# Expert weights loaded in other places, the first transposes copied amid the bias rows, one exponential for the last keys' bias, and more bias rows on ScalarE

## The chip, the cores and the metric

The kernel runs on one core of one Trainium2 chip. The metric is the time of one execution in device microseconds (us). TensorE is called PE here, its weight loads PEld, VectorE DVE, ScalarE ACT, GpSimd POOL; SP is the engine whose queue issues plain and transposing DMAs.

## The reference, cut to what matters

Attention over 8 sequences with 8 heads, 576 positions and 64 values a head, with a bias made of the distance of two positions; each row of the result (4,608 rows of 512 values) then goes through one of 8 experts, chosen by its domain.

```python
rel = pos[:, None] - pos[None, :]
x = (log1p(abs(rel)) / log1p(max(pos[:, None], 1)))[..., None]
bias = relu(x @ w1 + b1) @ w2                     # 576 x 576 x 8 heads
scores = q @ k.T / 8 + bias                       # for each sequence and head
rows = softmax(scores) @ v                        # 4608 x 512 after a transposition
for e in range(8):
    out[domain == e] = relu(rows[domain == e] @ moe_w1[e]) @ moe_w2[e]
```

## The kernel before, in words

**The bias.** It is the same for all sequences and made once, as its exponential. There are nine blocks: `hidden(ib)` makes 16 rows `hr` (each a 128x576 relu) on DVE (L202) or ACT (L199), and `outputs(ib)` multiplies them on PE with `W2BIG` into three PSUM tiles: query groups (0, 1) and (2, 3), 32 matmuls each (L221), and the last 64 keys, 16 matmuls (L225). ACT then takes exponentials into `biasM` (L237) and, for the last keys, into `biasR` (L234, two of them, one for each parity of the heads). `hidden(ib + 1)` is written ahead of `outputs(ib)`, so the rows of a block are made while PE works on the block before it. The ninth block is taken in pieces between score units of the first sequence (`LAST_ROWS`). Some fifty small routing operations of DVE (`next(route)`) also lie in this stretch and in the first sequence.

**The attention.** One round of `ROUND` for each sequence sets the order on PE, ACT and DVE by hand. A score unit (`m01`: head pair 0, key group 1) is two to eight matmuls into a ring of three PSUM tiles and one exponential on ACT (L560); `W..` multiplies by the bias on DVE (L571), `A..` multiplies with v on PE (L584, L588), `N.` divides by the sums on DVE (L614, L615). `T01`, `T23` transpose q and k of the next sequence on PE (L476), and `D..`, that is `take`, copies them out of PSUM (L506, on DVE). Those of the first sequence are made within the bias: (4,) after block 5, (0, 1) after block 6, (2, 3) after block 7, all through the one accumulator tile `pu`.

**The rows.** Rows of the result are scattered to a buffer in HBM, `fire_x`, sorted by expert (L645, on POOL: four DMAs of 128 rows, `xt`, and one of 64, `xl`, for each sequence). The scatters of a sequence are issued in the round after it.

**The experts.** An expert's weights are four quarters `w`, each 512 KB in SBUF after a cast in the DMA (L737, on POOL). There are 32; they go to a pool of 12 (`w_first`), to five of six tiles that held q, k and v (`n4`), and to a pool of 14 (`w_late`), whose first tile is used twice. `xA` is the first 512 rows of expert 0, fetched by a transposing DMA on SP before the last sequence is through (L952); `xT` are the other rows, expert by expert (L788, three buffers), and `ids` their destinations (L790). For each expert PE makes eight pairs of matmul groups (L799; expert 0: L809 with `xA`, L817 with the rest), ACT takes the relu (L839), PE multiplies with the second weights in five `second`s (L775, 40 matmuls), DVE copies each to a `res` tile (L778, eight buffers), and POOL scatters it to the output (L779).

**What sets the order.** POOL issues its DMAs strictly in the order in which they are written (`_Issue`), and a DMA of POOL waits for the one eight before it to have landed, since eight semaphores are used in turn. SP's queue is in order too. The calls `G.w.load(n, ...)` in `late` (by sequence `b` and unit number `ui`), at the head of `_phase_moe` and after each `second` say where the quarters stand in POOL's order.

Of the kernel before, what the change touches and what calls it, by code (L numbers as in the profile page):

```python
# [10 lines left out]
F16 = mybir.dt.float16  # L11
# [19 lines left out]
NSLOT = E * CAP + 128 * NOVF  # L31
PAD = 1 << 20
LN_EXP = 6
XW = DM + 2


# [25 lines left out]
""".split()  # L62


LAST_ROWS = {"m01": 1, "m03": 1, "m11": 2}


def rap(t, off, dims, nparts=None):
# [115 lines left out]
def _phase_bias(tc, G, route, at, x_dram):  # L184
# [4 lines left out]
    def hidden(ib, between=None):  # L189
        hrl = []  # L190
        for k16 in range(16):
            if ib < 8:
                r, a = ib // 2, 16 * (ib % 2) + k16
                m, c0 = 32 * r + a, C4 - (16 * a + r)
            else:
                m, c0 = 128 + k16, W4 + C1 - 4 * k16
            hr = fsb.tile([P, S], F16, tag="hr", name="hr", bufs=34)
            if k16 in ((2, 5, 8, 11, 14) if ib < 2 else (3, 8, 13) if ib % 2 == 0 else (5, 11)):
                nc.scalar.activation(out=hr, in_=G.L4[:, c0: c0 + S], func=AF.Relu,  # L199
                                     bias=G.pb1[:], scale=G.slope[:, m: m + 1])  # L200
            else:
                nc.vector.tensor_scalar(out=hr, in0=G.L4[:, c0: c0 + S],  # L202
                                        scalar1=G.slope[:, m: m + 1], scalar2=G.nb1[:],
                                        op0=AO.mult, op1=AO.max)
            hrl.append(hr)
            if (ib, k16) == (0, 7):
                G.slopes(16, NGR)
            if (ib, k16) in ((1, 1), (1, 5), (1, 9), (2, 1), (2, 5)):
                next(route)
            if between is not None and k16 == between[0]:  # L210
                at.take(0, between[1])
        return hrl

    def outputs(ib, hrl):
        for jcs in ((0, 1), (2, 3), (4,)):
            eb = G.ring()
            for k16 in range(16):
                for lj, jc in enumerate(jcs):
                    hr = hrl[k16]
                    if jc < 4:  # L220
                        nc.tensor.matmul(out=eb[:, lj, 32 * k16: 32 * k16 + 32],  # L221
                                         lhsT=rap(hr, jc, [[4, 128]]),
                                         rhs=G.W2BIG[:, 0:32], start=True, stop=True)
                    else:
                        nc.tensor.matmul(out=eb[0:64, lj, 32 * k16: 32 * k16 + 32],  # L225
                                         lhsT=hr[:, 512:576],
                                         rhs=G.W2BIG[:, 0:32], start=True, stop=True)
            ebv = eb.rearrange("p l (i h) -> p l h i", h=8)
            i0 = 64 * ib
            if jcs[0] == 4:  # L230
                for h2 in range(2):
                    o = G.biasR[64 * h2: 64 * h2 + 64, :, i0: i0 + 64] if ib < 8 else \
                        G.biasRL[64 * h2: 64 * h2 + 64]
                    nc.scalar.activation(out=o, in_=ebv[0:64, 0, h2::2, :],  # L234
                                         func=AF.Exp, bias=0.0, scale=0.125)
            elif ib < 8:
                nc.scalar.activation(out=G.biasM[:, jcs[0]: jcs[0] + 2, :, i0: i0 + 64], in_=ebv,  # L237
                                     func=AF.Exp, bias=0.0, scale=0.125)
# [10 lines left out]

    hrl = hidden(0)  # L250
    for ib in range(9):
        after = hidden(ib + 1, {6: (3, (4,)), 7: (9, (0, 1))}.get(ib)) if ib < 8 else None
        if ib == 1:
            nc.vector.memset(G.zero.rearrange("p o (r d) -> p (o r) d", r=4)[:, :, DM:].bitcast(I32), PAD)
            nc.sync.dma_start(out=x_dram.rearrange("(p c r) d -> p c (r d)", p=P, r=4),
# [3 lines left out]
                yield  # L259
        if ib == 0:  # L260
            next(route)
        if ib in (5, 6, 7):
            ps = {5: (4,), 6: (0, 1), 7: (2, 3)}[ib]
            at.transposes(0, ps, G.acc())
        if ib == 7:
            yield
        hrl = after
# [143 lines left out]
class _Attention:  # L411
# [85 lines left out]
    def take(self, b, ps):  # L497
        asb = self.G.asb
        if ps == (4,):
            t = self.qkTl[b] = asb.tile([P, 4, 2, 128], F16, tag="qkTl", name="qkTl", bufs=2)  # L500
            self.nc.vector.tensor_copy(out=t, in_=self.pt.pop((b, 4)))
        else:
            t = asb.tile([P, 2, 2, 512], F16, tag="qkT", name="qkT", bufs=4)
            for i, p in enumerate(ps):
                self.qkT[b, p] = t[:, i]
            self.nc.vector.tensor_copy(out=t.rearrange("p i x f -> p i (x f)"),  # L506
                                       in_=self.pt.pop((b, ps)).bitcast(F16))

    def scores(self, b, u):
        nc, G = self.nc, self.G  # L510
# [146 lines left out]
            self.load_vrag(b)  # L657

    def run(self, bias, route, late):
        units = [("r", 0)] + [("m", p, c) for p in (0, 1) for c in range(4)] + [("r", 1)] + \  # L660
                [("m", 2, c) for c in range(4)] + [("l", 0), ("l", 1), ("x",)] + \
                [("m", 3, c) for c in range(4)]
# [7 lines left out]
        def unit(b, name):  # L670
# [4 lines left out]
            if b == 0 and name in LAST_ROWS:  # L675
                for _ in range(LAST_ROWS[name]):
                    next(bias, None)
            if (b, name) == (0, "m00"):
                self.take(0, (2, 3))
            if b == 0 and ui > 2:  # L680
                for _ in range(2):
# [85 lines left out]
def _phase_moe(tc, G, moe_w1, moe_w2, x_dram, out):  # L767
# [50 lines left out]
                                 rhs=xT[:, dc, EARLY:], start=(dc == 0), stop=(dc == 3))  # L818
        nc.scalar.activation(out=hT[:, :, EARLY:], in_=hps, func=AF.Relu, bias=0.0, scale=1.0)

    G.w.load(2, G.n4)
    G.w.load(2, G.w_late)
    xTs = {e: fetch(e) for e in range(2)}
    novf = None
    for e in range(E):
# [62 lines left out]
def kernel(  # L888
# [24 lines left out]
    with tc.manual_schedule(engines={ET.PE, ET.DVE, ET.Activation}):  # L913
        with ExitStack() as att:
# [23 lines left out]
            def late(b, ui):  # L938
                if (b, ui) == (0, 7):
# [1 line left out]
                    G.bias_pools.close()  # L941
                    wsb = ctx.enter_context(tc.tile_pool(name="wsb", bufs=1, side="right", reuse_waits="tile"))
                    G.w_first = lambda name: wsb.tile([P, 2048], F16, tag="w", name=name, bufs=12)
                if b < 6 and ui == 10:
                    G.w.load(1, G.w_first)
                if (b, ui) in ((6, 1), (7, 5)):
                    G.w.load(3, G.w_first)
                if (b, ui) == (6, 3):
                    G.w.load(3, G.n4)
                if (b, ui) == (B - 1, 9):  # L950
                    G.early = G.n4("xA").rearrange("p (c t) -> p c t", c=4)
                    nc.sync.dma_start_transpose(out=G.early, in_=x_dram[0: EARLY, 0:DM])  # L952
# [36 lines left out]
```

## Time and profile before

| | |
|---|---|
| median of 3 runs | 398.47 us (397.8 to 398.48) |
| the profiled execution | 398.14 us, of which 396.6 us are the span from the first to the last instruction |
| busy in the span | PE 324.9 us (82%), ACT 246.9 (62%), DVE 236.6 (60%), PEld 214.2 (54%), POOL 182.5 (46%) |
| mean granted clock of TensorE | 0.956 of full speed |

The profiled execution is 1.54 us longer than its span and 0.33 us under the median. A share of busy time is a mean over three stages that have little in common: the bias to about 54 us, the attention to about 222 us, the experts to the end.

### The profile page before, as it was taken

To read this page: it belongs to the slowest core of one execution; us is meant where nothing else is said; L and a number is where in the kernel's file an instruction comes from. 1 tells how busy PE (TensorE), PEld (TensorE's weight loads), DVE (VectorE), ACT (ScalarE), POOL (GpSimd) and SP (SyncE) were. 2 spreads that over 40 slices of the span, in tenths; PEclk is the share of its full clock that TensorE was granted. 3 is DMA by queue.
4 is the path that set the end of the run, shared out by engine and by line. 5 is a ranking of instruction groups with operands and counts; after the bars stand their busy time and mean duration, and the time that the engine had idled before them with its cause. 6 is when DMAs were issued, how large, how long until landed. Compare 5 with 4: busy or idle time off the path is not lost.

```text
span 396.6 us, 9316 instructions
## 1 busy us (share of the span) xinstructions
PE 324.9 (82%) x3938; PEld 214.2 (54%) x3938; DVE 236.6 (60%) x440; ACT 246.9 (62%) x302; POOL 182.5 (46%) x220
## 2 busy tenths in 40 slices
PE   1599968789898989898787493999969985999893
PEld 1477846656566666565555243555536542656551
DVE  7999986999999999999889400212211202031211
ACT  8999968699999999999899040333214220514230
POOL 9250033049696969696445070836410046040312
PEclk9999988899999999999999697999989998999997
DMA  5999999039999999999966959999999259130302
GB/s 90 176 189 367 373 263 182 4 38 170 133 165 135 163 140 164 132 167 135 199 139 123 132 108 186 192 201 228 227 216 222 56 83 276 40 116 5 126 26 96
DMA packets 90996, 61.30 MB, mean 155 GB/s; under 512 B 43462, under 2 KB 85190, under 8 KB 90953
## 3 DMA queue, kind: packets, MB, share of 16 engines
q0 software_dynamic: 59904, 45.12, 69.2%
q1 hardware_dynamic: 31048, 15.57, 17.5%
q8 instruction: 31, 0.51, 0.5%
q14 instruction: 13, 0.10, 0.1%
HBM read 61.93 MB, written 24.70 MB: 218 GB/s over the span
## 4 chain that ended last, share of the span: by engine, by line
issue 24%; DVE 21%; DMA 19%; ACT 15%; PE 12%; POOL 6%; SPq 1%; POOLq 1%; DVEq 0%
ACT e L560 14%; DVE hr L202 7%; DMA out_dram<-res,ids 7%; DVE e L571 6%; POOL out_dram L779 5%; PE pu L588 4%; DMA w<-in_moe_w_dram 4%; DMA xA<-fire_x 3%; DMA ids<-fire_x 3%; DVE xt L615 2%; PE sc L532 2%; DVE qkT L506 2%; PE sc L476 2%; PE sc L538 1%; PE pu L584 1%
## 5 line engine op out<-in xcount | busy, mean ns | idle before, releaser
L560 ACT ACTIVATE e<-sc 128x1024 f16<-128x1024 f32 x168 | 152.2, 1019 | 13.1 <-PE sc L532 5.6
L778 DVE COPY res<-ops 128x512 f32<-128x512 f32 x40 | 27.6, 691 | 137.9 <-PE ops L775 126.8
L839 ACT ACTIVATE hT<-hps 128x640 f16<-128x640 f32 x56 | 39.4, 703 | 93.2 <-PE hps L799 76.1
L775 PE MATMUL ops<-w,hT 128*128 128x512 f16 x320 | 72.9, 387 | 5.3 <-DVE res L778 5.3
L571 DVE TENSOR_TENSOR e<-e,biasM 128x2048 f16<-128x2048 f16 x64 | 72.9, 1150 | 0.6 <-ACT e L560 0.4
L779 POOL DMA_INDIRECT out_dram<-res,ids x40 | 40.5, 1012 | 68.5 <-DVE res L778 48.7
L799 PE MATMUL hps<-xT,w 128*128 128x320 f16 x448 | 63.7, 304 | 5.3 <-DMA xT<-fire_x 4.3
L799 PEld LDWEIGHTS <-w 128*128 128x128 f16 x448 | 44.2, 99 | 25.2 <-issue 5.7
L532 PE MATMUL sc<-qkT 64*128 64x512 f16 x256 | 45.1, 385 | 15.0 <-ACT e L560 13.8
L775 PEld LDWEIGHTS <-hT 128*128 128x128 f16 x320 | 31.8, 100 | 43.6 <-issue 8.5
L645 POOL DMA_INDIRECT fire_x<-xt,posi x32 | 46.6, 1457 | 12.0 <-issue 8.2
L588 PE MATMUL pu<-vext,e 128*128 128x65 f16 x1024 | 48.1, 196 | 4.0 <-DVE e L571 4.0
L588 PEld LDWEIGHTS <-e 128*128 128x128 f16 x1024 | 43.4, 99 | 6.9 <-DVE e L571 5.0
L737 POOL DMA_DIRECT2D w<-in_moe_w_dram x32 | 27.7, 943 | 37.6 <-PE hps L799 32.2
L202 DVE TENSOR_SCALAR hr<-L,slope,nb 128x576 f16<-128x576 f16 x116 | 41.5, 427 | 0.0
L221 PE MATMUL sc<-W2BIG,hr 128*128 128x32 f16 x576 | 27.7, 193 | 13.1 <-DVE hr L202 9.6
L645 POOL DMA_INDIRECT fire_x<-xl,posi x8 | 10.4, 1296 | 52.8 <-DVE e L571 40.3
L221 PEld LDWEIGHTS <-hr 128*128 128x128 f16 x576 | 23.2, 116 | 17.8 <-DVE hr L202 14.1
L532 PEld LDWEIGHTS <-qkT 64*128 64x128 f16 x256 | 12.2, 93 | 35.5 <-issue 29.2
L584 PE MATMUL pu<-vrag,e 128*128 128x130 f16 x128 | 28.6, 223 | 2.2 <-DVE xl L631 1.4
L615 DVE TENSOR_TENSOR xt<-pu,rz 128x512 f16<-128x512 f32 (+1 forms) x33 | 22.3, 675 | 1.5
L199 ACT ACTIVATE hr<-L,pb,slope 128x576 f16<-128x576 f16 x28 | 22.2, 858 | 1.0 <-DVE slope L165 0.8
(128 smaller groups left out, 365.9 us busy)
## 6 DMA issues: line engine op xcount, KB each, us to landing
w<-in_moe_w_dram POOLq DMA_DIRECT2D x32, 512.0 KB
fire_x<-zero SPq DMA_DIRECT2D x1, 9252.0 KB
qn<-in_q_dram POOLq DMA_DIRECT2D x8, 512.0 KB
kn<-in_k_dram POOLq DMA_DIRECT2D x8, 512.0 KB
vst<-in_v_dram POOLq DMA_DIRECT2D x8, 512.0 KB
out_dram<-res,ids POOLq DMA_INDIRECT x40
last<-zero SPq DMA_DIRECT2D x2, 256.0 KB
last<-in_q_dram POOLq DMA_DIRECT2D x16, 32.0 KB
```

The source lines that it names most:

```text
L202: nc.vector.tensor_scalar(out=hr, in0=G.L4[:, c0: c0 + S], scalar1=G.slope[:, m: m + 1], scalar2=G.nb1[:], op0=AO.mult, op1=AO.max)
L221: nc.tensor.matmul(out=eb[:, lj, 32 * k16: 32 * k16 + 32], lhsT=rap(hr, jc, [[4, 128]]), rhs=G.W2BIG[:, 0:32], start=True, stop=True)
L532: mm(out=sc[:, h2, :], lhsT=self.qkT[b, p][hs[h2], 1, 128 * c: 128 * c + 128], rhs=self.qkT[b, p][hs[h2], 0, :], start=not raw, stop=True)
L560: nc.scalar.activation(out=ef[:, 0:n], in_=sf[:, 0:n], func=AF.Exp, bias=0.0, scale=0.125)
L571: self.nc.vector.tensor_tensor(out=job[0], in0=job[0], in1=job[1], op=AO.mult)
L584: mm(out=self.pu[:, c // 2, o: o + 130], lhsT=er[:, p % 2, 128 * c: 128 * c + 128], rhs=vr[:, p, :], start=True, stop=False, skip_group_ch ...
L588: mm(out=self.pu[:, c // 2, o + 65 * h2: o + 65 * h2 + 65], lhsT=self.e[b, ("m", p, j)][:, h2, 128 * c: 128 * c + 128], rhs=vx[:, 2 * p + ...
L645: inst = self.nc.gpsimd.indirect_dma_start(out=self.x_dram[:, :], out_offset=bass.IndirectOffsetOnAxis(ap=self.G.posi[0:n, c:c + 1], axis= ...
L775: nc.tensor.matmul(out=ops_, lhsT=hT[:, fc, t0: t0 + 128], rhs=G.w.w2(e, fc), start=(fc == 0), stop=(fc == 7))
L779: inst = nc.gpsimd.indirect_dma_start(out=out[:], out_offset=bass.IndirectOffsetOnAxis(ap=idx.bitcast(I32), axis=0), in_=res[:], in_offset ...
L799: nc.tensor.matmul(out=hps[:, i, 0:HC], lhsT=G.w.w1(e, dc, fc), rhs=xT[:, dc, HC * hf: HC * hf + HC], start=(dc == 0), stop=(dc == 3))
L839: nc.scalar.activation(out=hT[:, fc, :].rearrange("p (a b) -> p a b", a=2), in_=first(e, xT, ((fc, 0), (fc, 1))), func=AF.Relu, bias=0.0, ...
```

## The change

It has five parts. (1) The quarters of the weights stand elsewhere in POOL's order. Unit 10 of sequences 0 to 6 loads 4, 2, 1, 2, 1, 1 and 1 (it was one in each of sequences 0 to 5); three still go to `n4` at unit 3 of sequence 6, two more now at its unit 13. The three at unit 1 of sequence 6, the three at unit 5 of sequence 7 and the four at the head of `_phase_moe` are gone. So 17 quarters stand ahead of the experts where 15 and then four stood, and 15 behind `second`s where 13 did. (2) The first sequence's copy of (0, 1) stands after 2 rows of the ninth block, not 10; its transposes (2, 3) and their copy stand behind the score unit m01, not after block 7; the ninth block's pieces follow m03, m10 and m11, not m01, m03 and m11. (3) The last keys' matmuls are 32 of 16 columns, even heads to partitions 0 to 63 and odd heads to 64 to 127, and one exponential takes both. (4) Blocks 3, 5 and 7 give ACT three rows each instead of two. (5) The second transposes of sequence 1 are copied on ACT.

```diff
+W_FIRST = {0: 4, 1: 2, 2: 1, 3: 2, 4: 1, 5: 1, 6: 1}
-LAST_ROWS = {"m01": 1, "m03": 1, "m11": 2}
+LAST_ROWS = {"m03": 1, "m10": 1, "m11": 2}
...
-            if k16 in ((2, 5, 8, 11, 14) if ib < 2 else (3, 8, 13) if ib % 2 == 0 else (5, 11)):
+            if k16 in ((2, 5, 8, 11, 14) if ib < 2 else (3, 8, 13)):
...
-                        nc.tensor.matmul(out=eb[0:64, lj, 32 * k16: 32 * k16 + 32],
-                                         lhsT=hr[:, 512:576],
-                                         rhs=G.W2BIG[:, 0:32], start=True, stop=True)
+                        for h2 in range(2):
+                            nc.tensor.matmul(out=eb[64 * h2: 64 * h2 + 64, 0, 16 * k16: 16 * k16 + 16],
+                                             lhsT=hr[:, 512:576],
+                                             rhs=rap(G.W2BIG, h2, [[2, 16]]), start=True, stop=True)
...
-                for h2 in range(2):
-                    o = G.biasR[64 * h2: 64 * h2 + 64, :, i0: i0 + 64] if ib < 8 else \
-                        G.biasRL[64 * h2: 64 * h2 + 64]
-                    nc.scalar.activation(out=o, in_=ebv[0:64, 0, h2::2, :],
-                                         func=AF.Exp, bias=0.0, scale=0.125)
+                nc.scalar.activation(out=G.biasR[:, :, i0: i0 + 64] if ib < 8 else G.biasRL,
+                                     in_=eb[:, 0, 0:256].rearrange("p (i q) -> p q i", q=4),
+                                     func=AF.Exp, bias=0.0, scale=0.125)
...
-        after = hidden(ib + 1, {6: (3, (4,)), 7: (9, (0, 1))}.get(ib)) if ib < 8 else None
+        after = hidden(ib + 1, {6: (3, (4,)), 7: (1, (0, 1))}.get(ib)) if ib < 8 else None
...
-        if ib in (5, 6, 7):
-            ps = {5: (4,), 6: (0, 1), 7: (2, 3)}[ib]
-            at.transposes(0, ps, G.acc())
+        if ib in (5, 6):
+            at.transposes(0, (4,) if ib == 5 else (0, 1), G.acc())
...
+            if (b, ps) == (1, (2, 3)):
+                self.nc.scalar.copy(out=o, in_=i)
+            else:
+                self.nc.vector.tensor_copy(out=o, in_=i)
...
-            if (b, name) == (0, "m00"):
+            if (b, name) == (0, "m01"):
+                self.transposes(0, (2, 3), G.acc())
                 self.take(0, (2, 3))
...
-    G.w.load(2, G.n4)
-    G.w.load(2, G.w_late)
     xTs = {e: fetch(e) for e in range(2)}
...
-                if b < 6 and ui == 10:
-                    G.w.load(1, G.w_first)
-                if (b, ui) in ((6, 1), (7, 5)):
-                    G.w.load(3, G.w_first)
-                if (b, ui) == (6, 3):
-                    G.w.load(3, G.n4)
+                if ui == 10 and b in W_FIRST:
+                    G.w.load(W_FIRST[b], G.w_first)
+                if (b, ui) in ((6, 3), (6, 13)):
+                    G.w.load(3 if ui == 3 else 2, G.n4)
```

On POOL, from the scatters of sequence 6 to the first outputs, this stood before (`fire_x` is the row buffer, `out_dram` the output):

```order
L645 DMA fire_x<-xt,posi 9216x514 x4
L737 DMA w_4362<-in_moe_w_dram 128x4x512
L737 DMA w_4364<-in_moe_w_dram 128x4x512
L737 DMA w_4366<-in_moe_w_dram 128x4x512
L639 IOTA xt 128x4
L639 IOTA xl 64x1
L645 DMA fire_x<-xl,posi 9216x514
L645 DMA fire_x<-xt,posi 9216x514 x4
L737 DMA w_4677<-in_moe_w_dram 128x4x512
L737 DMA w_4679<-in_moe_w_dram 128x4x512
L737 DMA w_4681<-in_moe_w_dram 128x4x512
L737 DMA w_4683<-in_moe_w_dram 128x4x512
```

At the same place of the changed kernel stands:

```order
L647 DMA fire_x<-xt,posi 9216x514 x4
L641 IOTA xt 128x4
L641 IOTA xl 64x1
L647 DMA fire_x<-xl,posi 9216x514
L647 DMA fire_x<-xt,posi 9216x514 x4
L783 DMA out_dram<-res,ids 4608x512
L741 DMA w_4893<-in_moe_w_dram 128x4x512
L783 DMA out_dram<-res,ids 4608x512
```

The three loads behind sequence 6's scatters and the four behind sequence 7's are gone from there; the first load among the experts now stands behind the first output.

On POOL, at unit 10 of sequence 0, one load stood between the counters of the rows (IOTA) and the first scatter; in the changed kernel there are four:

```order
L641 IOTA xt 128x4
L641 IOTA xl 64x1
L741 DMA w_1683<-in_moe_w_dram 128x4x512
L741 DMA w_1685<-in_moe_w_dram 128x4x512
L741 DMA w_1687<-in_moe_w_dram 128x4x512
L741 DMA w_1689<-in_moe_w_dram 128x4x512
L647 DMA fire_x<-xl,posi 9216x514
```

The first scatter of sequence 0 and the loads of q and k of sequence 3 behind it now follow four loads.

On ACT, from the last full block of the bias into the first sequence, this stood before (`e` are the exponentials of scores, a number marks the tile that two units share):

```order
L199 ACTIVATE hr<-L_110,pb_89,slope 128x576 x3
L237 ACTIVATE biasM<-sc 128x16x64 x2
L234 ACTIVATE biasR<-sc 64x4x64 x2
L560 ACTIVATE e<-sc 128x1024
L560 ACTIVATE e_1288<-sc 128x1024 x2
L244 ACTIVATE biasL<-sc 128x4x2x64 x2
L560 ACTIVATE e_1336<-sc 128x1024 x2
L244 ACTIVATE biasL<-sc 128x4x2x64 x2
L560 ACTIVATE e_1391<-sc 128x1024 x2
L234 ACTIVATE biasRL<-sc 64x256 x2
```

Now stands there, down to the copy of part (5):

```order
L233 ACTIVATE biasR<-sc 128x4x64
L562 ACTIVATE e<-sc 128x1024
L562 ACTIVATE e_1375<-sc 128x1024 x2
L562 ACTIVATE e_1421<-sc 128x1024 x2
L244 ACTIVATE biasL<-sc 128x4x2x64 x2
L562 ACTIVATE e_1476<-sc 128x1024
L244 ACTIVATE biasL<-sc 128x4x2x64 x2
L562 ACTIVATE e_1476<-sc 128x1024
L233 ACTIVATE biasRL<-sc 128x256
L562 ACTIVATE e_1604<-sc 128x1024 x2
L562 ACTIVATE e<-sc 128x1024
L562 ACTIVATE e_1677<-sc 128x1024 x2
L507 COPY qkT<-sc 128x2048
```

Five exponentials of scores now come before the first piece of the ninth block, and a copy of 2,048 elements stands among those of the third head pair.

## Rows read from the trace of the kernel before

**Rows 1.** Busy time by stage: attention, first expert, experts 1 to 4.

```profile
core 0: us, PE busy (x) PEld busy (x) DVE busy (x) ACT busy (x) POOL busy (x), PEclk, DMA share, GB/s
82.00:222.50 140.50, 118.85 (x2048) 83.25 (x2044) 132.07 (x191) 131.85 (x147) 98.02 (x108) 1.00 1.00 146
222.50:253.80 31.30, 21.06 (x105) 10.79 (x105) 4.89 (x12) 5.12 (x5) 12.91 (x14) 0.79 0.94 147
253.80:336.40 82.60, 73.05 (x418) 41.55 (x417) 13.82 (x20) 22.50 (x32) 30.51 (x33) 0.96 1.02 190
```

**Rows 2.** Timeline of PE among the experts: start, length, instructions, [idle before, releaser].

```profile
221.89 0.60 PE L588 MATMUL pu<-vext,e 128*128 128x65 f16 x8
226.10 8.36 PE L809 MATMUL hps<-xA,w 128*128 128x512 f16 x32 [3.61 <-DMA xA<-fire_x]
234.30 3.62 PE L775 MATMUL ops<-w,hT 128*128 128x512 f16 x16
244.55 3.60 PE L817 MATMUL hps<-xT,w 128*128 128x128 f16 x32 [6.63 <-DMA xT<-fire_x]
253.76 8.86 PE L799 MATMUL hps<-xT,w 128*128 128x320 f16 x64
271.81 8.85 PE L799 MATMUL hps<-xT,w 128*128 128x320 f16 x64 [0.56 <-DMA xT<-fire_x]
293.01 10.53 PE L799 MATMUL hps<-xT,w 128*128 128x320 f16 x64 [3.71 <-DMA xT<-fire_x]
312.01 8.86 PE L799 MATMUL hps<-xT,w 128*128 128x320 f16 x64
331.32 5.20 PE L775 MATMUL ops<-w,hT 128*128 128x512 f16 x16 [5.28 <-DVE res L778]
336.36 8.86 PE L799 MATMUL hps<-xT,w 128*128 128x320 f16 x64
353.69 8.86 PE L799 MATMUL hps<-xT,w 128*128 128x320 f16 x64
```

**Rows 3.** Timeline of POOL, around the last scatters and the last load.

```profile
211.44 2.69 POOL L737 DMA_DIRECT2D w<-in_moe_w_dram  x3
...
226.88 0.95 POOL L645 DMA_INDIRECT fire_x<-xl,posi  x1 [12.49 <-DMA xA<-fire_x]
...
232.99 3.44 POOL L737 DMA_DIRECT2D w<-in_moe_w_dram  x4
...
321.17 0.76 POOL L737 DMA_DIRECT2D w<-in_moe_w_dram  x1 [32.19 <-PE hps L799]
```

**Rows 4.** DMA issues: queue, count, us from issue to landing.

```profile
xA<-fire_x SPq DMA_TRANSPOSE x1, 12.8
```

**Rows 5.** Timeline of DVE, the last division of the attention.

```profile
222.75 0.42 DVE L615 TENSOR_TENSOR xt<-pu,rz 128x256 f16<-128x256 f32 x1
```

**Rows 6.** DMA queues, 280 to 284 us: packets, MB, share of 16 engines.

```profile
q0 software_dynamic: 601, 0.78, 92.1%
q1 hardware_dynamic: 599, 0.15, 27.1%
```

**Rows 7.** DMA queues, 304 to 308 us.

```profile
q1 hardware_dynamic: 3750, 0.91, 115.3%
```

**Rows 8.** Busy time, clock and DMA from 70 to 82 us.

```profile
70.00:82.00 12.00, 9.81 (x142) 7.51 (x141) 11.86 (x19) 8.43 (x10) 0.00 (x0) 0.86 0.00 1
```

**Rows 9.** Timeline of DVE in the bias and the first sequence.

```profile
28.16 4.51 DVE L202 TENSOR_SCALAR hr<-L,slope,nb 128x576 f16<-128x576 f16 x13
...
64.42 1.22 DVE L506 COPY qkT<-sc 128x2048 f16<-128x2048 f16 x1 [2.64 <-PE sc L476]
...
72.23 1.22 DVE L506 COPY qkT<-sc 128x2048 f16<-128x2048 f16 x1
```

**Rows 10.** Timeline of ACT there.

```profile
50.20 0.75 ACT L234 ACTIVATE biasR<-sc 64x256 f16<-64x256 f32 x2
54.84 2.85 ACT L560 ACTIVATE e<-sc 128x1024 f16<-128x1024 f32 x3 [3.89 <-PE sc L538]
...
74.33 1.02 ACT L560 ACTIVATE e<-sc 128x1024 f16<-128x1024 f32 x1 [2.85 <-PE sc L545]
```

**Rows 11.** Timeline of PE, the last keys' matmuls of one block.

```profile
29.40 1.04 PE L225 MATMUL sc<-W2BIG,hr 128*64 128x32 f16 x16
```

More of the change, by code (lines that the diff above doesn't have):

```diff
@@ L505, in take @@
                 self.qkT[b, p] = t[:, i]
-            self.nc.vector.tensor_copy(out=t.rearrange("p i x f -> p i (x f)"),
-                                       in_=self.pt.pop((b, ps)).bitcast(F16))
+            o, i = t.rearrange("p i x f -> p i (x f)"), self.pt.pop((b, ps)).bitcast(F16)
+            if (b, ps) == (1, (2, 3)):
+                self.nc.scalar.copy(out=o, in_=i)
+            else:
+                self.nc.vector.tensor_copy(out=o, in_=i)
     def scores(self, b, u):
@@ L659, in run @@
     def run(self, bias, route, late):
+        G = self.G
         units = [("r", 0)] + [("m", p, c) for p in (0, 1) for c in range(4)] + [("r", 1)] + \
```

## The prediction

> **What bounds the kernel now.** I read the busy time by stage first. In the attention, 82 to 222.5 us, ACT is busy for 131.85 of 140.5 us, DVE for 132.07 [rows 1]. That stage is bound by its engines, and the change leaves its instructions as they are. Among the experts only PE could bind, and there it loses time twice: it is busy for 21.06 of 31.30 us with expert 0 and for 73.05 of 82.60 us with experts 1 to 4, and the granted clock falls to 0.79 and 0.96 of full speed, so part of that is PE at the lower of its two levels [rows 1]. The timeline of PE says what it waits for [rows 2]: 3.61 us for `xA`, 6.63 us for expert 0's other rows, 0.56 and 3.71 us for the rows of experts 2 and 3, 5.28 us for a result tile. An undisturbed expert takes 353.69 - 336.36 = 17.33 us; the steps before it take 18.05, 21.20, 19.00 and 24.35 us.
>
> What is late behind these waits stands on POOL and in the queues. Three quarters of weights are issued at 211.44 us, just ahead of `xA`, which then takes 12.8 us to land [rows 3, 4]. The last sequence's scatters wait 12.49 us for `xA` to have been read, since they write the same buffer. Behind them come four more quarters at 232.99 us, and the fetch of expert 0's other rows starts amid these. The last quarter waits 32.19 us for a tile, and every output behind it waits too [rows 3].
>
> **The change part by part.** A quarter is 0.524 MB. With both queues full, POOL's queue q0 moved 0.78 MB in 4 us, so a quarter costs 2.7 us of it [rows 6].
>
> (1) `xA`, -3.6 us. Without the three quarters it has the queues almost to itself. Its 0.52 MB would take 2.3 us at the 0.91 MB in 4 us that q1 moved alone [rows 7]. With a start and an end of 1 to 2 us I estimate 5 us, where it took 12.8. PE has it at 226.10, so it is issued near 213.3 us, 9 us before PE ends the attention at 222.49 [rows 2]; the whole 3.61 us go; the other bound is nothing, if the 12.8 us have another cause.
>
> (2) Expert 0's other rows, -7.9 us. The five scatters take 232.99 - 226.88 = 6.1 us of POOL. They can begin when `xA` has been read, at about 220 us; the last two wait for the division that ends at 223.17 us [rows 5]. I put their end at 226.5 us, 6.5 us earlier, and the fetch with it at about 228. No load is in flight then, so 128 rows land in 3 us or so, by 231. PE comes there at 222.49 + 8.36 + 3.62 = 234.5 us, so 6.63 us of wait go, with 3 us to spare. The stretch from 244.55 to 253.76 us is 9.21 us, begun at the lower clock after that idle time. At full clock its 24 second matmuls are 24 of the 40 that take 17.33 - 8.86 = 8.47 us, so 5.1; the 32 short ones I put between 1.8 (half of 3.60) and 3.6, near 2.9. That gives 8.0 and -1.2. Bounds 0 and -8.6. Expert 1 begins near 242.2.
>
> (3) Experts 1 to 3, -6.3 us: three steps at 17.33 are 52.0 where 58.25 stand (253.76 to 312.01). This holds if each `xT` lands in time. From 228 us q1 runs alone until POOL has issued the first output and the first load behind it. That is when PE's first `second` is through and copied, near 233.5, so the load's data come near 236. In 8 us q1 alone moves 1.8 MB; expert 0's rest, expert 1 and half of expert 2 are 1.1. The remaining half then goes at 0.15 MB in 4 us [rows 6], 9 us, to 245, and is wanted at 259.5. Expert 3's rows, 17.5 us each at that pace, come near 263, wanted at 276.9; expert 4's near 281, wanted at 294.2. Bounds 0 and -6.3.
>
> (4) Expert 4, -7.0 us. Before, the last quarter stands behind expert 2's third `second`; seven results are queued behind it, of eight tiles. Now it stands behind the fifth, and five are queued, so three tiles are free when expert 4's `second`s start. The first tile came back at most 331.32 - 321.17 = 10.15 us after POOL went on [rows 2, 3]; the fourth result of expert 4 would then be copied some 3 us late, on DVE. PE has two PSUM tiles for results and then 8.86 us of expert 5's first matmuls, so it doesn't wait. 24.35 becomes 17.33. Bounds 0 and -7.0.
>
> (5) The bias and the first sequence, -3.5 us. DVE gives up three rows of 4.51 / 13 = 0.35 us, 1.0 us together, and a copy of 1.2 us at 72.23; a wait of 2.64 us at 64.42, for transposes that stand behind pieces of the ninth block, should shrink as ACT starts earlier [rows 9]. From 70 to 82 us DVE is busy for 11.86 of 12 us [rows 8], so what DVE gains here carries to the first full round. ACT's first score exponential waits 3.89 us, idle, for matmuls behind the copy that moves [rows 10]. ACT takes on three rows, the copy (two exponentials of 1,024 would be 1.9 us) and loses nine of 0.38 us; it has 3.89 and 2.85 us of idle time to hold that. DVE's certain part is 2.2, with all of the wait 4.8; I take half of the wait. Low end: +1.0, if the copy of 1.9 us on ACT delays scores and the wait stays.
>
> The last keys' matmuls are part of that bound. 16 took 1.04 us [rows 11]; 32 of half the width take between 1.04 and 2.08. PE waits for rows of DVE in every block, so only those of the last full block stand ahead of the first score unit: 0 to +1.0 us. The Trainium skill (TensorEngine Tiling (Array Packing), Instruction Overhead) says that a matmul of one column lasts as long as one of 60; by it the 32 take 2.08 us, and the sum is 1.0 us longer. The same page (Key Properties) lets different column tiles work in parallel, which would give 1.04 and change nothing; no row of this trace shows halves of 16 columns.
>
> The moved loads I cost at nothing. In sequence 0 three more are 8 us of q0; the DMA engines do nothing from 72 to 82 us, and POOL has nothing to issue [rows 8]. In sequences 1 and 3 one more is 2.7 us in a round of 20 (140.5 us hold seven); the DMA share is 1.00 there and 1.19 with both queues full [rows 1, 6], some 3 us free in a round. What these loads could delay, q, k and v, is wanted a round later. Without that cover each costs 2.7 us.
>
> Sum: -3.6 - 7.9 - 6.3 - 7.0 - 3.5 = -28.3; 398.14 - 28.3 = 369.8, and against the median, 0.3 above the profiled execution, 370.1 us.
>
> **The rivals.**
> *The transposes stay starved.* Packets of q0 and q1 go one for one, 601 to 599, and q1's are a fifth as large [rows 6]; experts 2 and 3 were 21.2 us apart, near the 17.5 us of one fetch. If loads fill q0 before expert 1's rows are in, that pace holds for two steps: 2 x (21.2 - 17.33) = +7.7, 377.8 us. Against it: q1 has 8 us to itself. The Trainium skill (DMA: Bandwidth & Descriptors, Queues, rings and completion order) says that each engine takes queues in turn, packet by packet; the trace agrees, 601 to 599. By that rule alone any step with loads in flight goes at 21 us.
> *The last quarter still stops the outputs.* If its tile or the results come back later than I think, (4) gives nothing: 377.1 us.
> *Only expert 0 gains.* If (3), (4) and half of (5) fail together, because 15 loads behind `second`s are two more than before and keep q0 full: 398.5 - 11.5 - 1.7 = 385.3 us.
> *Slower.* Loads beside q, k and v make the attention wait for DMA. To cost more than the 28 us, each of seven rounds would have to be 4.1 us longer, more than a load's 2.7. The DMA share of 1.00 leaves too little backlog for that, unless POOL, in order and eight DMAs deep, falls a whole round behind.
>
> **How the numbers follow.** Forecast 0.58, range 365 to 374 from the ends of (5) and a miss of 3 us among the experts. Transposes 0.17, last quarter 0.08, only expert 0 0.10, no change 0.02, slower 0.05. A measurement of this kernel tells 0.2%, 0.8 us, from no change. So faster 0.93, within 0.2% 0.02, slower 0.05. 365 to 380 us holds the first three, 0.83.
>
> **What would show it.** `xA` landing in about 5 us and no idle time of PE before L813's group of `xA` (L809 before); the other rows' matmuls without a wait; experts 17.3 us apart throughout; no idle PE in expert 4; the first score exponential near 51 us; an attention of 140 us from its second sequence on, as before. The prediction is wrong if a round grows by 2 us or more, if expert 1's rows land after 243 us, or if PE waits for a result tile.

## The result and the profile after

The changed kernel took 372.98 us as a median of four executions (367.99 to 390.59), the kernel before 398.13 beside it. The ratio is 0.927, interval 0.922 to 0.933, which is 369.2 us; it counts the executions of 367.99 and 370.48 us. All ratios here leave out executions over 1.5% above the fastest of the same kernel: half or more of those of the changed kernel here and of front_only, last_early, four_back, mixed and even, which lie up to 33 us above it. The profiled execution is the one of 375.47 us (span 373.5, 1.97 outside).

Busy time, clock and DMA by stage, the columns of [rows 1]: attention, expert 0, experts 1 to 4, and expert 4 alone.

```profile
82.00:219.40 137.40, 117.17 (x2027) 82.19 (x2025) 130.30 (x187) 129.75 (x144) 97.40 (x109) 1.00 1.03 151
219.40:236.60 17.20, 17.20 (x105) 8.71 (x104) 4.90 (x12) 5.12 (x5) 9.54 (x11) 1.00 0.71 115
236.60:313.10 76.50, 72.26 (x418) 41.67 (x417) 13.14 (x19) 22.53 (x32) 27.92 (x30) 0.96 1.25 193
292.90:313.00 20.10, 20.05 (x104) 11.36 (x105) 2.08 (x3) 5.63 (x8) 6.26 (x7) 0.86 1.21 169
```

Expert 0's stage shrank from 31.3 to 17.2 us, all of it PE's work at a granted clock of 1.00 (0.79 before). The DMA engines are no emptier in experts 1 to 4: a share of 1.25, where it was 1.02. The timeline of PE, which answers to [rows 2]:

```profile
219.22 7.07 PE L813 MATMUL hps<-xA,w 128*128 128x512 f16 x32
226.13 3.62 PE L779 MATMUL ops<-w,hT 128*128 128x512 f16 x16
229.58 1.95 PE L821 MATMUL hps<-xT,w 128*128 128x128 f16 x32
...
236.55 8.86 PE L803 MATMUL hps<-xT,w 128*128 128x320 f16 x64
253.88 8.86 PE L803 MATMUL hps<-xT,w 128*128 128x320 f16 x64
271.22 8.85 PE L803 MATMUL hps<-xT,w 128*128 128x320 f16 x64
292.95 11.66 PE L803 MATMUL hps<-xT,w 128*128 128x320 f16 x64 [4.24 <-DMA xT<-fire_x]
313.08 8.86 PE L803 MATMUL hps<-xT,w 128*128 128x320 f16 x64
```

The waits for `xA`, for expert 0's other rows and for a result tile are gone. One has come: 4.24 us for expert 4's rows, and behind it a group of 11.66 us, 2.8 more than the others, in a stretch of clock 0.86. Without these 7.0 us the span would be 366.5. The two executions that the ratio counts had 366.0 and 368.5, which fits, but neither was profiled.

POOL, to [rows 3]; then `xA` from issue to landing, to [rows 4]; then SP's issues of the fetches for experts 2 to 4, and the last of these from issue to landing (the DMA issues of 262 to 280 us):

```profile
217.77 0.92 POOL L647 DMA_INDIRECT fire_x<-xl,posi  x1 [9.61 <-DVE xl L633]
...
223.04 0.97 POOL L647 DMA_INDIRECT fire_x<-xt,posi  x1 [0.30 <-issue]
229.76 1.00 POOL L783 DMA_INDIRECT out_dram<-res,ids  x1 [5.75 <-DMA ids<-fire_x]
...
304.92 0.79 POOL L741 DMA_DIRECT2D w<-in_moe_w_dram  x1 [17.69 <-PE hps L803]
```

```profile
xA<-fire_x SPq DMA_TRANSPOSE x1, 5.1
```

```profile
230.68 7.60 SPq L792 DMA_TRANSPOSE xT<-fire_x  x1
...
239.05 20.28 SPq L792 DMA_TRANSPOSE xT<-fire_x  x1
...
260.31 20.83 SPq L792 DMA_TRANSPOSE xT<-fire_x  x1
```

```profile
xT<-fire_x SPq DMA_TRANSPOSE x1, 32.5
```

`xA` lands in 5.1 us, the scatters wait for their own data, not for `xA`, and end at 224.0 us. Expert 4's fetch starts only at 260.31, behind one that held SP for 20 us, and holds SP as long itself. Its rows land 32.5 us after its issue, at 292.8, which is 11.7 us after SP was through with it.

In the bias and the first sequence, ACT, PE and DVE (to [rows 9 to 11]):

```profile
49.69 0.38 ACT L233 ACTIVATE biasR<-sc 128x256 f16<-128x256 f32 x1
50.65 1.94 ACT L562 ACTIVATE e<-sc 128x1024 f16<-128x1024 f32 x2 [0.57 <-PE sc L540]
53.86 1.02 ACT L562 ACTIVATE e<-sc 128x1024 f16<-128x1024 f32 x1 [1.27 <-PE sc L534]
```

```profile
29.37 1.02 PE L227 MATMUL sc<-W2BIG,hr 128*64 128x16 f16 x32
```

```profile
55.71 1.22 DVE L509 COPY qkT<-pu 128x2048 f16<-128x2048 f16 x1 [2.55 <-PE pu L475]
...
79.98 0.87 DVE L633 TENSOR_TENSOR xl<-pu,rz 64x256 f16<-64x256 f32 x2
```

The first score exponential comes at 50.65 us (54.84 before), the last division of sequence 0 at 79.98 (82.15 before), the end of the attention at 219.39 (222.49).

### The profile page after: what moved, and what is told of

Read it like the earlier page. It is cut to its first block, busy times and chain, and to the rows that moved or that the text cites. A ratio compares the mean times of both kernels' runs of the same rounds, so it can differ in the third digit from the quotient of the medians.

```text
span 373.5 us, 9583 instructions
## 1 busy us (share of the span) xinstructions
PE 318.8 (85%) x4082; PEld 210.8 (56%) x4082; DVE 234.9 (63%) x436; ACT 247.8 (66%) x297; POOL 181.4 (49%) x220
## 5 line engine op out<-in xcount | busy, mean ns | idle before, releaser
L779 PE MATMUL ops<-w,hT 128*128 128x512 f16 x320 | 70.5, 379 | 0.0
L803 PE MATMUL hps<-xT,w 128*128 128x320 f16 x448 | 64.8, 307 | 5.3 <-DMA xT<-fire_x 4.2
L647 POOL DMA_INDIRECT fire_x<-xt,posi x32 | 45.8, 1433 | 11.0 <-issue 8.8
L222 PE MATMUL sc<-W2BIG,hr 128*128 128x32 f16 x576 | 26.7, 193 | 12.3 <-DVE hr L203 9.7
L222 PEld LDWEIGHTS <-hr 128*128 128x128 f16 x576 | 22.4, 116 | 17.0 <-DVE hr L203 12.9
L200 ACT ACTIVATE hr<-L,pb,slope 128x576 f16<-128x576 f16 x31 | 24.5, 859 | 0.8 <-DVE slope L166 0.8
```

The costliest lines, as they stand in the source:

```text
L222: nc.tensor.matmul(out=eb[:, lj, 32 * k16: 32 * k16 + 32], lhsT=rap(hr, jc, [[4, 128]]), rhs=G.W2BIG[:, 0:32], start=True, stop=True)
L647: inst = self.nc.gpsimd.indirect_dma_start(out=self.x_dram[:, :], out_offset=bass.IndirectOffsetOnAxis(ap=self.G.posi[0:n, c:c + 1], axis= ...
L779: nc.tensor.matmul(out=ops_, lhsT=hT[:, fc, t0: t0 + 128], rhs=G.w.w2(e, fc), start=(fc == 0), stop=(fc == 7))
L803: nc.tensor.matmul(out=hps[:, i, 0:HC], lhsT=G.w.w1(e, dc, fc), rhs=xT[:, dc, HC * hf: HC * hf + HC], start=(dc == 0), stop=(dc == 3))
```

## The experiments

They ran in four groups, each beside the kernel before. The first (weights_only, front_only, spread, last_early) and the second (changed_again, three_back, four_back, late_more) ran on one chip, the three mixed ones on another, even on a third. The kernel before took 401.47, 399.83, 401.32 and 398.08 us beside them. A ratio is against the kernel before in the same group. Two marks are read from every profile: "round 1", from the last division of sequence 0 to that of sequence 1 on DVE (19.44 us before and after), and the end of the attention on PE.

**weights_only.** Before, with part (1) alone.

```diff
+W_FIRST = {0: 4, 1: 2, 2: 1, 3: 2, 4: 1, 5: 1, 6: 1}
...
-    G.w.load(2, G.n4)
-    G.w.load(2, G.w_late)
...
```

> The kernel before with part (1) alone: the quarters of weights as in the changed kernel, the bias and the first sequence as before. Theory: the two halves of the change add up. The attention ends at 222.5 us as before (222.49), the experts take what they take in the changed kernel (its span less 219.39 us), so the time is 3.1 us over the changed kernel's: 371 to 374 us where no fetch is late, 378 to 379 where expert 4's rows come some 4 us late as in the profiled execution. No idle PE ahead of the xA group. Rival: the quarters moved into sequences 0 to 6 hold up q, k and v, and the attention then ends over 0.5 us later than 222.5 us; the changed kernel's front gained more than 3.1 us and lost some of it to the loads.

384.59 us, ratio 0.957 (0.952 to 0.962). PE doesn't wait for `xA` or the other rows, but the attention ends at 225.8 us: round 1 takes 22.59 us. The rival holds in its effect. Among the experts ACT stands still in expert 5, and PE behind it for 4.41 us:

```profile
315.45 0.70 ACT L838 ACTIVATE hT<-hps 128x640 f16<-128x640 f32 x1 [9.48 <-PE hps L800]
321.11 1.30 ACT L838 ACTIVATE hT<-hps 128x640 f16<-128x640 f32 x2 [4.95 <-remote]
```

**front_only.** The changed kernel with the quarters in their old places.

```diff
+    G.w.load(2, G.n4)
+    G.w.load(2, G.w_late)
...
-                if ui == 10 and b in W_FIRST:
-                    G.w.load(W_FIRST[b], G.w_first)
...
+                if b < 6 and ui == 10:
+                    G.w.load(1, G.w_first)
+                if (b, ui) in ((6, 1), (7, 5)):
+                    G.w.load(3, G.w_first)
...
```

> The changed kernel with the quarters where the kernel before has them: parts (2) to (5) alone. Theory: the attention ends at 219.4 us and all that follows moves with it, waits included: 3.6 us for xA, about 6.6 for expert 0's other rows, about 5 for a result tile. 395.0 us, 3.1 under before (ratio 0.992). Rival: the loads behind which xA and the other rows stand are set by DMA and don't move up with the engines, so the waits grow by what the front gains: 397.5 to 398.5 us, and PE waits 6 to 7 us for xA.

Ratio 0.976 (0.969 to 0.983): 9.5 us less than before, three times the theory's 3.1. But it rests on three of seven executions (391.06 to 393.08 us); the median of all seven, 397.91 us, is 3.6 us less than before. So what the front is worth by itself stays open. The profile is of the slowest of them (404.4 us span) and can't say more; it does show the waits for `xA` (4.33 us) and the other rows (5.08) unchanged in kind, and round 1 at 19.46 us. The ratios of the two halves multiply to 0.934, the changed kernel has 0.947 on this chip; they don't add up, and that stays open.

**last_early.** The changed kernel with the last quarter in its old place.

```diff
-            G.w.load(1, G.w_late)
+            G.w.load(3 if (e, kk) == (2, 2) else 1, G.w_late)
```

> The changed kernel, but the last three quarters all stand behind expert 2's third second, so that the very last one stands where it stood before the change, ahead of seven results that wait for it, not five. By the prediction's step (4) PE then waits about 5.3 us for a result tile in the second matmuls of expert 4 (5.28 before), and the time is 5 us over the changed kernel's: 373 to 376 us where its own is 368 to 370.5. Rival: the place of the last quarter didn't matter, since results come back faster with fewer loads behind them: no wait of PE for a result tile, the same time as the changed kernel within 1 us.

Ratio 0.958 (0.951 to 0.965), some 4 us above the changed kernel's 0.947. In the profiled execution (394.25 us) PE waits for result tiles in experts 3 and 4, and POOL stands before the last load:

```profile
301.13 3.57 PE L779 MATMUL ops<-w,hT 128*128 128x512 f16 x8 [4.84 <-DVE res L782]
...
325.35 5.50 PE L779 MATMUL ops<-w,hT 128*128 128x512 f16 x16 [6.42 <-DVE res L782]
```

```profile
314.05 0.74 POOL L741 DMA_DIRECT2D w<-in_moe_w_dram  x1 [12.38 <-PE hps L803]
```

The wait that the prediction's step (4) removes comes back when the quarter does.

**changed_again.** The changed kernel, unaltered.

> The changed kernel itself, unaltered, beside the other three. What the first experiments showed: the three kernels with the new places of the loads ended the attention at 225.6 to 226.9 us, the one with the old places at 220.6, the changed kernel's first profile at 219.4. Theory: the early loads put DMA so close to full that PE now and then stands without an instruction in a round (idle time put down to no semaphore, at the transposes of sequence 1 above all), so this run too shows one to three rounds of 21.5 to 22.7 us among the 19.57, and an attention that ends at 221 to 227 us; with a late fetch among the experts 374 to 382 us in all. Rival: that was of those three kernels and not of the loads; the rounds are 19.6 each, the attention ends at 219.4 us, and the time is 368 to 375.5 us.

378.51 us (377.11 to 381.57), ratio 0.947 (0.944 to 0.951), with the attention ending at 224.9 us. Rounds 1 and 6 take 22.91 and 21.49 us, those between 19.57. No fetch is late here, and experts 1 to 3 take 17.33 us each; in expert 5 PE waits 2.29 and 0.92 us for ACT, which stood 2.83 us as in weights_only. With the same loads, expert 2's fetch starts 1.1 us ahead of the first load (236.75 against 237.88) and holds SP for 3.15 us; in the first profile it starts with that load (230.68 against 230.74) and takes 7.60. That this start decides it isn't shown. In round 1 PE stops inside the transposes of sequence 2:

```profile
90.26 0.24 PE L475 MATMUL sc<-idn,qn 128*64 128x128 f16 x1 [0.27 <-issue]
90.27 0.34 PE L475 MATMUL sc<-idn,kn 128*64 128x128 f16 x4
91.00 0.32 PE L475 MATMUL sc<-idn,kn 128*64 128x128 f16 x4 [0.39 <-issue]
```

These take 0.4 us for eight elsewhere; "issue" says that no semaphore held PE. So it isn't q, k or v that come late at this stop. The four groups of eight take 2.2 us in place of 1.1, ACT then stands 1.92 us for PE, and from 92 to 96 us the granted clock is 0.60, where the first profile has 1.00.

**three_back.** The changed kernel, with three of sequence 0's four quarters loaded ahead of `xA` again.

```diff
-W_FIRST = {0: 4, 1: 2, 2: 1, 3: 2, 4: 1, 5: 1, 6: 1}
+W_FIRST = {0: 1, 1: 2, 2: 1, 3: 2, 4: 1, 5: 1, 6: 1}
...
+                if (b, ui) == (7, 5):
+                    G.w.load(3, G.w_first)
```

> The changed kernel, but three of the four quarters of sequence 0 stand at unit 5 of sequence 7 again, ahead of xA. By the prediction's step (1): xA takes about 12 us to land, and PE waits 3.6 us for it (3.61 before, 4.33 with the old places and the new front) and comes out of the wait at the lower clock; the five scatters wait for xA, the other rows start 6 us later. 3.6 to 8 us over the changed kernel. If the four loads in sequence 0 are what held PE up in sequence 1, that round takes 19.6 us here. Rival: xA's 12.8 us had another cause, it lands in 5 to 8 us and PE doesn't wait; no difference.

384.65 us (ratio 0.962, 0.959 to 0.966), 6.1 over the changed kernel beside it. `xA` takes 13.1 us, and PE waits:

```profile
225.42 9.71 PE L813 MATMUL hps<-xA,w 128*128 128x512 f16 x32 [3.36 <-DMA xA<-fire_x]
```

Step (1) holds. The 6.1 us are not all its own: the profiled executions differ by 3.7, and 1.9 of that is a longer expert 5. And round 1 takes 19.46 us: with one load in sequence 0 in place of four, PE's stop is gone.

**four_back.** The changed kernel, with four quarters at the head of the experts again.

```diff
-                if (b, ui) in ((6, 3), (6, 13)):
-                    G.w.load(3 if ui == 3 else 2, G.n4)
+                if (b, ui) == (6, 3):
+                    G.w.load(3, G.n4)
...
+    G.w.load(2, G.n4)
+    G.w.load(2, G.w_late)
     xTs = {e: fetch(e) for e in range(2)}
...
-            G.w.load(1, G.w_late)
+            if (e, kk) > (0, 1):
+                G.w.load(1, G.w_late)
```

> The changed kernel, but four quarters stand again at the head of the experts, behind the last scatters: two are taken from unit 13 of sequence 6, and nothing is loaded behind the first two seconds, so that all later loads stand where the changed kernel has them. By the prediction's step (2): the fetch of expert 0's other rows, issued near 226 us, runs beside 2.1 MB of loads, takes near 10 us, and PE waits 4 to 6 us for it, with a lower clock behind: 5 to 8 us over the changed kernel. Rival: the scatters' earlier end alone was what counted, and the fetch lands before PE comes (229.6 us) or within 1 us of it; the same time within 1.5 us, or less, since expert 1 and 2 have two loads less in front of them.

380.18 to 389.86 us, too wide for a ratio. The wait for the other rows is back (5.09 us, 6.63 before), and the group behind it is slow again; expert 0's stage is 5.5 us longer than in changed_again. Step (2) holds. The two lowest executions, 380.18 and 381.77 us, are 1.7 and 3.3 above the changed kernel's 378.51, where 5 to 8 was expected; the profile has 1.7 us back in expert 5.

```profile
239.57 3.43 PE L821 MATMUL hps<-xT,w 128*128 128x128 f16 x32 [5.09 <-DMA xT<-fire_x]
```

**spread.** Three loads for each of experts 0 to 4, not five for each of experts 0 to 2; on weights_only's chip.

```diff
-            G.w.load(1, G.w_late)
+            if kk % 2 == 0:
+                G.w.load(1, G.w_late)
```

> The changed kernel, with the 15 quarters among the experts loaded behind the first, third and fifth second of experts 0 to 4, not behind each of the first fifteen. Theory (POOL's queue full of loads holds the transposing fetches at some 20 us each): with 3 loads, about 8 us of q0, in each 17.33 us, every fetch is through in well under 17 us; no PE wait for xT of any expert, full clock from 219 us on, the last load waits for no tile. Span 366 us, 367 to 368 us in all executions, and a narrower spread than the changed kernel's 368 to 375. Rival: the fetches are slow beside the scatters of results or by themselves, whatever the loads do: SP's issue of a fetch still takes 18 to 20 us, expert 4 or 5 waits for its rows, 370 to 376 us. A second rival: the quarters of experts 5 and 6 now come late, and PE waits for w.

375.19 us (374.26 to 376.26), ratio 0.934 (0.930 to 0.938): 3 us below changed_again on the same chip, 5 by the ratios; this version beats the changed kernel there. From expert 1 on, PE has no wait for rows, weights or ACT; the steps are 17.33 us. The attention ends at 225.7 us (round 1: 21.93, round 6: 22.68), which takes what the forecast of 367 to 368 had. One part of the theory falls: the queues are no emptier. From 245 to 300 us the DMA share is 1.27 here, 1.28 after, 1.24 before, although 175 GB/s were moved here and 198 and 212 there. What changed is SP's time with the fetches for experts 3 and 4: 12.54 and 9.84 us, where the changed kernel's first profile has 20.28 and 20.83.

**late_more.** Five quarters fewer in the attention, 20 among the experts, four for each of experts 0 to 4.

```diff
+W_FIRST = {0: 1, 1: 1, 2: 1, 3: 1, 4: 1, 5: 1, 6: 1}
...
+            if kk != 2:
+                G.w.load(1, G.w_first if (e, kk) < (1, 1) else G.w_late)
```

> A version meant to be better: one quarter in each of sequences 0 to 6 (so 12 with the five in n4, not 17), and 20 among the experts, four for each of experts 0 to 4, none behind the third second; nothing ahead of xA or of the scatters. Theory: with the lighter load the attention's rounds stay at 19.57 us and it ends at 219.4 us; among the experts 4 loads are 10.8 us of q0 in 17.33, so fetches come in time; no PE wait for xT or w, span 366 us, 367 to 369 us, below the changed kernel and below the version with three loads an expert where that lost time in the attention. Rival: with four loads an expert q0 is full enough to starve the transposing fetches (20 us each, as with five), and expert 3 or 4 waits 4 us or more for rows: 371 to 376 us.

Ratio 0.940 (0.935 to 0.944). Both the theory's rounds and the rival's fetches came: rounds 1 to 6 take 19.45 to 19.61 us, and the fetches for experts 3 to 6 hold SP for 20.4 to 21.0 us each. PE then waits for a quarter in expert 5 and for rows in expert 6.

```profile
310.11 11.53 PE L803 MATMUL hps<-xT,w 128*128 128x320 f16 x64 [4.20 <-DMA w<-in_moe_w_dram]
...
332.60 10.53 PE L803 MATMUL hps<-xT,w 128*128 128x320 f16 x64 [2.33 <-DMA xT<-fire_x]
```

**mixed, mixed_old_order, mixed_two_exp.** The loads of late_more, but four for experts 0 and 1 and three for experts 2 to 5; then that with part (2) undone, and with part (3) undone.

```diff
+            if kk in ((0, 1, 3, 4) if e < 2 else (0, 2, 4)):
```

> A version put together from the runs so far: one quarter in each of sequences 0 to 6, as where all rounds took 19.57 us, and behind the seconds of the experts four each for experts 0 and 1 and three each for experts 2 to 5 (20 in all), as where no fetch was late. Theory (DMA near its limit is what costs: in the attention through PE standing without an instruction, among the experts through fetches of 20 us): attention ends at 219.4 us, experts 17.33 us apart, no wait for xT or w; span about 366 us, 367 to 369 us, a ratio near 0.92, under the changed kernel on this chip (0.947) and the version with three loads an expert (0.934). Rival: two fetches of 20 us at the start, beside four loads an expert, already put expert 4 or 5 late by 2 to 4 us, or the last quarters, loaded in expert 5, come late for expert 7: 371 to 375 us.

> The run labelled mixed, with part (2) undone: the copies, transposes (2, 3) and pieces of the ninth block where the kernel before has them. By the prediction's step (5) this part carries most of the front's gain: the last division of sequence 0 (79.5 to 80.5 us with the new front, 82.2 to 82.6 with the old) goes back by 1.5 to 2.5 us, and the first score exponential waits near 4 us again. Rival: the gain is DVE's three rows and the smaller ACT work, and this part gives under 0.7 us.

> The run labelled mixed, with part (3) undone: 16 matmuls of 32 columns and two exponentials of 64 partitions for the last keys. PE's time doesn't change (1.04 us for 16, 1.02 us for 32 of half the width, by the traces so far); ACT has 9 x 0.38 = 3.4 us more in the bias. Theory: ACT is busy for 19.1 of 20 us from 30 to 50 us, so it can't hold that and four rows too; the last division of sequence 0 comes 1 to 2.5 us later. Rival: DVE bounds the bias (busy for all of these 20 us), ACT's 3.4 us are hidden, 0 to 0.5 us.

mixed ran from 370.72 to 403.62 us, too wide for a ratio. Its loads are those of mixed_old_order, which took 371.61 us (ratio 0.927, 0.922 to 0.931) without a wait among the experts, and of mixed_two_exp (0.951, 0.945 to 0.956), which waited 6.81 us for expert 6's weights. From 245 to 300 us mixed_old_order and mixed_two_exp did the same work (first the one, then the other, by busy time; then PE's wait in mixed_two_exp):

```profile
245.00:300.00 55.00, 55.00 (x336) 32.70 (x334) 10.37 (x15) 18.74 (x28) 24.13 (x25) 1.00 1.26 208
```

```profile
245.00:300.00 55.00, 55.00 (x336) 32.68 (x335) 10.37 (x15) 18.88 (x27) 24.13 (x25) 1.00 1.26 194
```

```profile
334.31 10.17 PE L804 MATMUL hps<-xT,w 128*128 128x320 f16 x64 [6.81 <-DMA w<-in_moe_w_dram]
```

The DMA engines were as busy, but moved 208 GB/s in one and 194 in the other. Which transfer is late among the experts thus hangs on a rate that differs between executions of kernels with the same code there. On the front: the last division of sequence 0 stands at 80.68 us in mixed, 80.29 with the old order, 80.93 with two exponentials; ten profiles of the new front lie between 79.55 and 80.68. The old front has 82.15 before and 82.64 in weights_only. So the order gives nothing to be seen here, although ACT's first score exponential waits 4.32 us again without it; the second expectation's rival holds, and the third can't be told from its own. Parts (4) and (5), in which DVE gives up three rows and a copy, were not undone by themselves; which part brings the 2 to 3 us isn't shown.

**even.** spread, with the 12 loads of `w_first` dealt out evenly.

```diff
-W_FIRST = {0: 4, 1: 2, 2: 1, 3: 2, 4: 1, 5: 1, 6: 1}
+W_FIRST = {0: 2, 1: 2, 2: 2, 3: 2, 4: 2, 5: 1, 6: 1}
```

> The version with three loads for each of experts 0 to 4 (spread), whose loads in the attention are dealt out more evenly: two in each of sequences 0 to 4, one in 5 and 6, not 4, 2, 1, 2, 1, 1, 1. It tells whether what held the attention up was the four loads together in sequence 0 or the number of loads in it. Theory (the four together): round 1 takes 19.6 us, not 21.5 to 22.9, the attention ends near 220 to 221.5 us, the experts follow 17.33 us apart without a wait, 369 to 371 us, a ratio of 0.92 to 0.925 where spread had 0.934 and the changed kernel 0.947. Rival (the number): 17 quarters in the attention fill DMA wherever they stand, one or two rounds take 21.5 us or more, the attention ends at 223 to 226 us, 372 to 376 us.

Ratio 0.928 (0.925 to 0.932). The profiled execution (369.46 us) has rounds of 19.44 to 19.83 us, an end of the attention at 219.7 us with 17 quarters loaded in it, and no wait among the experts. That agrees with the theory, but doesn't show it: even ran on another chip than changed_again, and the changed kernel's first profile, with four together, has a round 1 of 19.44 us too. On the first chip, three_back (one in sequence 0, 14 by sequence 6) kept its round 1 and four_back (four in sequence 0, 15 by sequence 6) did not, so there it hung on sequence 0's loads and not on the total. Against the changed kernel's first 0.927, 0.928 is no gain that can be shown.

## Why the prediction was right, point by point

The forecast of 370.1 us stands against 369.2; the profiled execution against its own sum: front -3.1, expert 0 -14.1, experts 1 to 3 -1.9, expert 4 -4.2, the rest +0.6, together -22.7 us of 398.14.

That 370.1 and 369.2 us are so near is in part luck: the two executions behind 369.2 were not profiled, and in the profiled one expert 0 gained 2.6 us more than forecast and experts 1 to 4 gained 7.2 less. On the chip of the first two groups the same kernel has 0.947 (0.944 to 0.951), which is 377.1 us against 398.13 and outside the range of 365 to 374, and round 1 is 3.5 us longer, one of the prediction's own signs of being wrong.

(1) and (2), `xA` and expert 0's other rows: right in mechanism, by three_back and four_back each undone by itself. -14.1 us (31.27 to 17.16, from 219.39 to 236.55) where -11.5 was forecast, 1.9 beyond the bounds (-3.6 and -8.6; with the 1.8 us that it allows the short matmuls, the second should be -8.9): the `xA` group, begun without a wait, took 7.07 us and not 8.36, and the 32 short matmuls 1.95, where 2.9 was taken as near the middle. The granted clock in these groups was 1.00; before, it was 0.84 and 0.50. The rows came by 229.6, earlier than the 231 forecast.

(3), experts 1 to 3: the term of -6.3 was worth -1.9 in the profile, since the third step holds the wait for expert 4's rows. The step that failed is "expert 4's near 281, wanted at 294.2". SP was through with that fetch at 281.1; but the working took a fetch as landed after its 17.5 us at 0.15 MB in 4 us [rows 6], and the rows landed 32.5 us after the issue, at 292.8. And they were wanted at 288.7, since expert 1 began at 236.55 and not near 242.2. This is the rival "the transposes stay starved", at 7.0 us with the slow clock behind (7.7 forecast), in one step and not two. changed_again, spread and even have all of the 6.3, so this kernel has the late fetch in one profile and not in the other.

(4), the last quarter: right, by last_early; no wait for a result tile after. Its -7.0 shows as -4.2, for the 2.8 us of lower clock that belong to (3).

(5), the front: -3.1 against -3.5, and the first score exponential came near 51 us as forecast. But the reason is not carried: the order of the copies, to which the removed waits were credited, gave nothing when undone, and DVE's wait of 2.64 us came back as one of 2.55 in front of the copy that was moved. PE's matmuls cost nothing: 32 in 1.02 us, 16 before in 1.04. By the Trainium skill (TensorEngine Tiling (Array Packing), Key Properties) different tiles work in parallel, and the trace agrees; by its section Instruction Overhead they would have taken 2.08 us, an estimate from the 1.04, and the trace does not agree. No run tells parallel tiles from a time that simply goes with the number of columns.

The moved loads, at nothing: right in the first profile, where round 1 is 19.44 us, and wrong on the chip of the first two groups. All five profiles there with four loads in sequence 0 have a round 1 of 21.9 to 22.9 us; the seven experiments' profiles with one or two, three of them on that chip, have 19.44 to 19.46. The cover named (idle DMA from 72 to 82 us, q, k and v wanted a round later) holds, and yet the loads cost 2.5 to 3.5 us by a way that the prediction didn't have: PE standing without a semaphore to wait for, a round after them, in some executions with a lower clock behind. Why a burst that ends before 82 us does this at 89 isn't settled. The rival "slower" needed 4.1 us in each round; in changed_again it was 3.5 us in one, and 1.9 in round 6, of which the kernel before has 1.2 too.

## What to carry over

Where DMA is full for 70 us on end, ask of each load not what it costs but which transfer stands behind it: the same bytes gave 14 us when `xA` and the last scatters no longer stood behind seven quarters. Count a fetch to its landing: here that came 11.7 us after SP was through with it. Deal loads out evenly: three in an expert were better than five on one chip, two in a round lost nothing in even, the one run that has them in five sequences. Leave a late quarter slack for a DMA rate that differs by 7% between executions. And measure again before a number is believed: 0.927 came back as 0.947. A wait taken off an engine that isn't the bound, as ACT's 3.9 us here, is no gain until another run shows it.

## What the runs showed of the hardware

- ACT stood 2.83 and 4.95 us in front of a relu, put down to "remote": a semaphore ended the wait, but the profile names nobody for it. In the trace it is the semaphore that PE's matmuls raise. In weights_only it rose at 321.08 us, though the last of these matmuls is recorded as ended at 316.04. Why it rose late isn't shown.
- In changed_again PE stood 0.27 and 0.39 us at a time amid transposes ("issue"), with no semaphore to wait for. Instructions come over the same DMA engines as data (32 packets of `q8`, 0.5% of their time, on the page after); whether they came late isn't shown, and full engines alone don't tell: from 88 to 92 us the DMA share was 1.34 in changed_again, which stops, and 1.38 in three_back, which doesn't.
- The same transfers at the same DMA share (1.26) ran at 194 GB/s in mixed_two_exp and 208 in mixed_old_order, on one chip.
- A transposing fetch of 0.66 MB held SP's queue 2.53 us with no load in flight, and 20.28 and 20.83 us behind loads (all in the first profile of the changed kernel). The first landed 4.8 us after its issue, the last 32.5.
